# Loading the first slice of w1 as two column pieces on two queues, in a SiLU MLP's forward and backward kernel

## The chip, the cores and the metric

The kernel runs on one core of a Trainium2 chip. The metric is the device time of one execution in microseconds (us). The time before is the median of five executions, 322.19 us (320.18 to 322.25). One execution was profiled: it took 321.06 us by the same clock, and its trace spans 319.3 us from the first to the last instruction, so 1.76 us lie around the span.

## The reference

A two-layer network with a SiLU between, and its gradients for a given `grad_out`. All tensors are bfloat16; S = 2048 rows, D = 640, F = 1536.

```
def _fwd_reference(x, w1, w2):          # x [1, 2048, 640], w1 [640, 1536], w2 [1536, 640]
    h = jnp.einsum("bsd,df->bsf", x, w1)
    h = _silu(h)
    out = jnp.einsum("bsf,fd->bsd", h, w2)
    return out

def reference(x, w1, w2, grad_out):
    _out, _vjp = jax.vjp(_f, x, w1, w2)  # _f is _fwd_reference
    _grads = _vjp(grad_out)
    return (_out, *_grads)               # out, grad x, grad w1, grad w2
```

## The kernel before

All matmuls are 128 by 128 stationary tiles, with D as five tiles (`DT` = 5), F as twelve (`FT` = 12) and S as sixteen. The rows of x are worked through in four chunks of 512 (`SC`). For each chunk the kernel computes h transposed (F on the partitions), SiLU and its derivative, then the gradient that comes back through w2, and then two products that give the chunk of `out` and of grad x; the two weight gradients come at the end, after all chunks. TensorE does all of this in one long sequence.

The change touches only the start, where nothing is on the chip yet. Chunk 0 has its own routine, `h_first`. The first three 128-row tiles of x (`NQ` = 3, 160 KB each) are loaded as they lie, and TensorE turns them (`pe_x`, line 211) with 15 transposes. Their results are copied from PSUM into `xT` (line 216) by VectorE, ScalarE and VectorE again: D tile 0, then D tiles 1 and 2, then 3 and 4. The fourth x tile is transposed by a DMA (line 195).

Then `h_first` runs its matmuls in an order that follows the loading of w1 (line 251). For each D tile `dt_` in turn, it multiplies `xT[:, dt_, 0:384]` with the first eight F tiles (`NA` = 8, `FA` = 1024 columns). So the first eight matmuls read only D tile 0 of w1, columns 0 to 1023, that is "the first w1 slice"; the next eight read D tile 1, and so on. 40 such matmuls are followed by 40 short ones over the last 128 rows, and then by F tiles 8 to 11 in the usual order (line 220).

w1 therefore comes in pieces: for each D tile one transfer of 128 rows by 1024 columns (`load_w1`, line 188; 256 KB), and one transfer for columns 1024 to 1535 of all D tiles (line 196). w1 and w2 go into `w1_nat` and `w2_nat`; the profile calls both `w_nat`. It calls the slice's transfers L188, the x tiles' L185, and it counts the DMA instructions on the queue of the engine that issues them, SPq for SyncE and ACTq for ScalarE.

What sets the order of the issues is the order in the code, engine by engine. ScalarE issues x tile 1 and then the first w1 slice. SyncE issues x tiles 0 and 2, then the w1 slices of D tiles 1 to 4, then the transposing load of the fourth x tile (line 195), the rest of w1 (line 196), w2 (line 199), the transposed `grad_out` chunk (line 179), the three parts of w2 transposed (line 202) and w1 transposed (line 203). `start_before_entry_wait` moves every engine's instructions up to the last one in the list `early` ahead of the wait at the program's entry; on SyncE that list ends with the slice of D tile 2. A DMA instruction may also wait for an earlier transfer: the semaphores of transfers are used again, in turn.

Of the kernel before, what the change touches and what calls it, by code (L numbers as in the profile page):

```python
# [75 lines left out]
def kernel(  # L76
# [11 lines left out]
    nc = tc.nc  # L88
# [13 lines left out]
    FC = 512  # L102
# [7 lines left out]
    FA = NA * P  # L110
# [37 lines left out]
    with ExitStack() as mctx:  # L148
# [9 lines left out]
        early = [nc.vector.memset(warm[:], 1.0)]  # L158
# [25 lines left out]
        def load_x(eng, q):  # L184
            return eng.dma_start(out=x_nat[:, q, :], in_=x_v[:, q, :])  # L185

        def load_w1(k, cols=slice(0, F), eng=nc.sync):
            return eng.dma_start(out=w1_nat[:, k, cols], in_=w1_v[:, k, cols])  # L188

        early += [load_x(nc.sync, 0), load_x(nc.scalar, 1), load_x(nc.sync, 2)]  # L190
        early += [load_w1(0, slice(0, FA), nc.scalar)]
        early += [load_w1(k, slice(0, FA)) for k in range(1, 3)]
        for k in range(3, DT):
            load_w1(k, slice(0, FA))
# [288 lines left out]
```

## Time and profile before

| What | Value | Where from |
|---|---|---|
| median of five executions | 322.19 us | 320.18, 321.06, 322.19, 322.24, 322.25 |
| the profiled execution | 321.06 us | one of the five |
| its span | 319.3 us | first to last instruction of the trace |
| TensorE (PE) busy | 314.7 us, 99% of the span | busy time by engine |
| VectorE / ScalarE busy | 102.9 / 77.2 us | busy time by engine |
| mean rate of the DMA engines | 209 GB/s | 66.85 MB over the span |
| first w1 matmul (line 251) starts | 5.89 us | timeline |
| last one of line 251 ends | 14.79 us | chain of waits |

A row of the timeline gives the start from the span's beginning, the duration of the run of equal instructions, the engine, the line, the operation and its tiles, how many there were, and in brackets how long the engine had been idle and what released it. For a DMA the row is the issue, on its issuing engine's queue; when the data have landed is told separately, as the time from issue to landing. The 16 DMA engines are shared by all queues: q10 carries what ScalarE issues and q1 what SyncE issues, and the share of a queue is the time of its packets as a part of 16 engines' time.

### The profile page before, as it was taken

The numbers are of one execution on the slowest core, as the hardware profiler recorded it, in microseconds if no ns is written. First come the engines' busy times: TensorE is split into PE (matmuls) and PEld (weight loads), VectorE is DVE, ScalarE is ACT, GpSimd is POOL, SyncE is SP. The second block draws the span as 40 slices with busy tenths as digits, with TensorE's granted clock in tenths as the row PEclk, the third lists the DMA queues.
The fourth block names the chain that finished last, engine by engine and source line by source line (L and its number), as shares of the span: only waits on it lengthen the run. The fifth ranks groups of instructions, "written<-read, shape, count | busy, mean of one in ns | idle before, by whom it ended". The sixth has DMA issues, their size and how long they took to land.

```text
span 319.3 us, 3632 instructions
## 1 busy us (share of the span) xinstructions
PE 314.7 (99%) x1529; PEld 147.2 (46%) x1529; DVE 102.9 (32%) x182; ACT 77.2 (24%) x139; POOL 0.7 (0%) x6
## 2 busy tenths in 40 slices
PE   7999999999999999999999999999999999999997
PEld 5644444444444444444444444444444444444444
DVE  1388541477510087710147751000000110001001
ACT  2392001545201255411054520110100001001010
POOL 0000000000000000000000000000000000000000
PEclk9999999999999999999999999999999999999999
DMA  8999999999799684291635079909999999996011
GB/s 245 349 177 233 234 269 267 330 298 313 214 288 311 171 204 121 73 321 66 165 120 147 0 245 271 226 19 300 259 231 261 258 218 344 267 235 210 33 35 49
DMA packets 147120, 66.85 MB, mean 209 GB/s; under 512 B 113312, under 2 KB 146464, under 8 KB 147104
## 3 DMA queue, kind: packets, MB, share of 16 engines
q1 hardware_dynamic: 146816, 66.20, 81.6%
q10 hardware_dynamic: 288, 0.43, 0.4%
q8 instruction: 12, 0.20, 0.3%
q14 instruction: 4, 0.03, 0.0%
HBM read 9.18 MB, written 28.97 MB: 119 GB/s over the span
## 4 chain that ended last, share of the span: by engine, by line
PE 97%; DMA 2%; ACTq 0%; issue 0%; DVE 0%; DVEq 0%
PE hp L299 32%; PE hp L388 16%; PE hp L283 16%; PE hp L439 15%; PE hp L220 14%; PE hp L251 3%; DMA w_nat<-in_w_dram 2%; PE hp L419 1%; ACTq L185 0%; DVE g L430 0%; DVEq L430 0%; ACTq L467 0%
## 5 line engine op out<-in xcount | busy, mean ns | idle before, releaser
L283 PE MATMUL hp<-goT,w2T 128*128 128x512 bf16 x240 | 56.9, 379 | 0.0
L299 PE MATMUL hp<-aT,w_nat 128*128 128x512 bf16 x240 | 52.5, 379 | 0.0
L299 PE MATMUL hp<-ghT,w1T 128*128 128x512 bf16 x240 | 52.5, 379 | 0.0
L388 PE MATMUL hp<-a_blk,go_nat 128*128 128x512 bf16 x240 | 52.0, 379 | 0.0
L439 PE MATMUL hp<-gh_blk,x_nat 128*128 128x512 bf16 x224 | 48.5, 379 | 0.0
L220 PE MATMUL hp<-xT,w_nat 128*128 128x512 bf16 x200 | 48.2, 379 | 0.0
L307 ACT ACTIVATE oT<-hp 128x512 bf16<-128x512 f32 x24 | 14.4, 599 | 104.3 <-PE hp L299 104.3
L229 ACT ACTIVATE aT<-hp 128x512 bf16<-128x512 f32 x48 | 28.5, 613 | 38.4 <-PE hp L220 30.4
L299 PEld LDWEIGHTS <-w_nat 128*128 128x128 bf16 x240 | 23.5, 98 | 28.3
L299 PEld LDWEIGHTS <-w1T 128*128 128x128 bf16 x240 | 23.5, 98 | 28.3
L388 PEld LDWEIGHTS <-go_nat 128*128 128x128 bf16 x240 | 23.5, 98 | 28.3
L283 PEld LDWEIGHTS <-w2T 128*128 128x128 bf16 x240 | 23.5, 98 | 28.3
L290 DVE SCALAR_TENSOR_TENSOR ghT<-ghT,hp 128x512 bf16<-128x512 bf16 x48 | 32.5, 683 | 7.0 <-PE hp L283 7.0
L439 PEld LDWEIGHTS <-x_nat 128*128 128x128 bf16 x224 | 21.9, 98 | 26.4
L309 DVE CAST oT<-hp 128x512 bf16<-128x512 f32 x16 | 11.0, 691 | 70.6 <-PE hp L299 70.6
L236 DVE SCALAR_TENSOR_TENSOR ghT<-aT,v 128x512 bf16<-128x512 bf16 x48 | 32.6, 687 | 0.3
L220 PEld LDWEIGHTS <-w_nat 128*128 128x128 bf16 x200 | 19.5, 98 | 23.4
L235 DVE TENSOR_SCALAR v<-t 128x512 bf16<-128x512 f32 x48 | 20.1, 426 | 28.1 <-ACT t L233 28.1
L233 ACT ACTIVATE t<-hp 128x512 f32<-128x512 f32 x44 | 26.4, 618 | 0.0
L450 DVE CAST g<-hp 128x512 bf16<-128x512 f32 x7 | 4.8, 692 | 47.0 <-PE hp L439 28.5
L398 DVE CAST g2T<-hp 128x512 bf16<-128x512 f32 x7 | 4.8, 692 | 46.1 <-PE hp L388 46.1
L396 ACT ACTIVATE g2T<-hp 128x512 bf16<-128x512 f32 x8 | 4.8, 598 | 47.0 <-PE hp L388 47.0
(24 smaller groups left out, 42.1 us busy)
## 6 DMA issues: line engine op xcount, KB each, us to landing
aT_scr<-aT SPq DMA_DIRECT2D x4, 1536.0 KB, 6.7
ghT_scr<-ghT SPq DMA_DIRECT2D x4, 1536.0 KB, 7.9
out_dram<-o_sb SPq DMA_DIRECT2D x8, 640.0 KB, 3.4
oT_scr<-oT SPq DMA_DIRECT2D x4, 640.0 KB, 3.9
go_nat<-in_grad_out_dram SPq DMA_DIRECT2D x4, 640.0 KB, 7.6
gxT_scr<-oT SPq DMA_DIRECT2D x4, 640.0 KB, 4.8
w_nat<-in_w_dram SPq DMA_DIRECT2D x1, 1920.0 KB, 10.4
x_nat<-in_x_dram SPq DMA_DIRECT2D x3, 640.0 KB, 7.0
```

What stands on the lines that cost most here:

```text
L220: nc.tensor.matmul(hp[:], lhsT=w1_nat[:, dt_, ft * P:(ft + 1) * P], rhs=xT[:, dt_, :], start=(dt_ == 0), stop=(dt_ == DT - 1),)
L229: nc.scalar.activation(aT[:, ft, :], hp[:], ACT.Silu)
L233: nc.scalar.activation(t[:], hp[:], ACT.Tanh, scale=0.5)
L235: nc.vector.tensor_scalar(out=v[:], in0=t[:], scalar1=-0.5, scalar2=0.5, op0=ALU.mult, op1=ALU.add)
L236: nc.vector.scalar_tensor_tensor(out=ghT[:, ft, :], in0=aT[:, ft, :], scalar=1.0, in1=v[:], op0=ALU.subtract, op1=ALU.mult)
L283: nc.tensor.matmul(gp[:], lhsT=w2T[:, dt_, ft * P:(ft + 1) * P], rhs=goT[:, dt_, :], start=(dt_ == 0), stop=(dt_ == DT - 1),)
L290: nc.vector.scalar_tensor_tensor(out=ghT[:, ft, :], in0=ghT[:, ft, :], scalar=1.0, in1=gp[:], op0=ALU.add, op1=ALU.mult)
L299: nc.tensor.matmul(op_[:], lhsT=w_all[:, ft, dt_ * P:(dt_ + 1) * P], rhs=rhs_all[:, ft, :], start=(ft == 0), stop=(ft == FT - 1),)
L307: nc.scalar.activation(oT[:, dt_, :], op_[:], ACT.Copy)
L309: nc.vector.tensor_copy(out=oT[:, dt_, :], in_=op_[:])
L388: nc.tensor.matmul(gp[:], lhsT=go_nat[:, st, dt_ * P:(dt_ + 1) * P], rhs=a_blk[:, st, :], start=(st == 0), stop=(st == ST - 1),)
L439: nc.tensor.matmul(gp[:], lhsT=x_nat[:, st, dt_ * P:(dt_ + 1) * P], rhs=gh_blk[:, st, :], start=(st == 0), stop=(st == ST - 1),)
```

## The change

```
-        early += [load_w1(0, slice(0, FA), nc.scalar)]
+        early += [load_w1(0, slice(0, FC), nc.scalar), load_w1(0, slice(FC, FA))]
         early += [load_w1(k, slice(0, FA)) for k in range(1, 3)]
         for k in range(3, DT):
             load_w1(k, slice(0, FA))
```

`FC` is 512 and `FA` is 1024. The first slice, 128 rows by 1024 columns, becomes two transfers of 128 rows by 512 columns (128 KB each). Columns 0 to 511 stay on ScalarE's queue behind x tile 1. Columns 512 to 1023 go on SyncE's queue, behind x tile 2, which is the third x tile, and ahead of the slices of D tiles 1 to 4. Both are in the list `early`. No other transfer, no matmul and no copy is changed.

More of the change, by code (lines that the diff above doesn't have):

```diff
@@ L190 @@
         early += [load_x(nc.sync, 0), load_x(nc.scalar, 1), load_x(nc.sync, 2)]
-        early += [load_w1(0, slice(0, FA), nc.scalar)]
+        early += [load_w1(0, slice(0, FC), nc.scalar), load_w1(0, slice(FC, FA))]
         early += [load_w1(k, slice(0, FA)) for k in range(1, 3)]
```

## The prediction

> **What bounds the kernel now.** I read the chain of waits first, in order of time, then TensorE's own waits.
>
> ```profile
> 0.63 5.22 DMA w_nat<-in_w_dram
> 5.84 0.04 issue
> 5.89 8.91 PE hp L251 x80
> 14.79 4.32 PE hp L220 x20
> ```
>
> ```profile
> PE hp L251 <- DMA w_nat<-in_w_dram: 1.8, 1, 1.8
> PE wp L162 <- DVE warm L158: 0.5, 1, 0.5
> ```
>
> The reader is to see two things. From 5.89 us to the end TensorE (PE) waits for nothing: its list of waits has only these two entries, both ahead of that. So whatever moves the matmuls of line 251 earlier or later moves the end by as much, until some other load comes late. And what they wait for is one transfer, the first w1 slice: issued at 0.63, landed at 5.84.
>
> Was the other operand ready? The timeline around 4 us:
>
> ```profile
> 2.62 1.51 PE L211 MATMUL tp<-ident,x_nat 128*128 128x128 bf16 x15
> 3.95 0.82 DVE L216 COPY xT<-tp 128x384 bf16<-128x384 bf16 x2 [3.50 <-PE tp L211]
> 4.06 0.80 ACT L216 COPY xT<-tp 128x768 bf16<-128x768 bf16 x1 [1.37 <-PE tp L211]
> ```
>
> Yes. VectorE's first copy takes 0.36 us (the shorter of that group's two, 358 and 548 ns), so D tile 0 of x stands at 4.31 and all of it at 4.86. The w1 slice is 1.53 us later than its partner.
>
> Why so late? The DMA queues in two stretches, 2.4 to 3.8 us and 3.8 to 5.6 us (packets, MB, share of 16 engines):
>
> ```profile
> q10 hardware_dynamic: 144, 0.25, 56.9%
> q1 hardware_dynamic: 150, 0.21, 45.6%
> ...
> q1 hardware_dynamic: 237, 0.44, 81.3%
> q10 hardware_dynamic: 8, 0.01, 3.9%
> ```
>
> The slice is the last transfer on q10. Nearly all of it moved before 3.8 us; in the next 1.8 us only eight packets of q10 went. 128 rows over 16 engines are eight per engine, so I read the tail as one DMA engine that was held up and then shared its turns with q1. The transfer lands when that engine has finished.
>
> **What the change does, part by part.**
>
> *The half on ScalarE's queue.* Same issue slot (0.63), half the bytes. It lands at 5.84 at the latest if the engine is held up as before. At best it is ready before xT is, and F tiles 0 to 3 start at 4.31 + 0.04 = 4.35. The 40 long matmuls take 6.51 us (the stretch from 5.89 to 12.40), 0.163 each, so these four take 0.65 and the eight of one D tile 1.30. Before, D tile 1 began at 5.89 + 1.30 = 7.19; that is the point to compare with.
>
> *The half on SyncE's queue.* It takes the slot at 1.00 that D tile 1's slice had; every later issue of SyncE moves back one slot. The four slices were issued at 1.00, 1.48, 2.04 and 2.42 and took 5.1, 5.3, 5.3 and 5.6 us to land: 6.1, 6.8, 7.3 and 8.0. This is the row nearest to the new transfer: same queue, same place behind x tile 2, twice the bytes. Two bounds follow.
>
> - *Every slot lands as it did, whatever is in it.* The new half at 6.1, D tile 1 at 6.8. F tiles 4 to 7 run from 6.14 to 6.79, D tile 1 starts at 6.84: **0.35 us earlier** than 7.19.
> - *The bytes decide.* Ahead of D tile 1's slice there are the same bytes as before, so it lands at 6.1 still. The new half, ahead of it on the same queue, is there by then minus its successor's share; if it and the first half are ready by 4.8, D tile 1 starts at 6.14: **1.05 us earlier**. The far bound is xT alone, 4.35 + 1.30 = 5.65, or 1.54 earlier, which would need D tile 1's slice to land 0.5 us sooner than it did. I don't take that for the estimate; it marks the floor.
>
> *Costs.* The additional issue takes about the row's 0.43 us on SyncE (slots 0.47 apart) and holds up nobody but SyncE's own later loads. Moved by 0.47, with TensorE 1.05 earlier, they stand thus. D tiles 2, 3 and 4 in the next slots (7.3, 8.0, some 8.7) against needs at 7.44, 8.74 and 10.04. The transposed fourth x tile, 2.95 + 5.8 + 0.47 = 9.2, against 11.35. The rest of w1, 4.29 + 6.4 + 0.47 = 11.2, against 13.6. All are covered, D tile 2 by a tenth only; if that cover is gone, its lateness comes off the gain and no more. The rows of the packets are shorter: 1280-byte packets cost 54 ns (182 packets at 102% of 16 engines over 0.6 us) and 2048-byte ones 84 ns (124 at 93% over 0.7 us), so I estimate 45 ns for 1024 bytes. 256 x 45 / 16 = 0.72 us instead of 128 x 84 / 16 = 0.67: 0.05 us, inside the bounds.
>
> *The wait that moves.* SyncE's queue itself waits once in this stretch:
>
> ```profile
> SPq L199 <- DMA w_nat<-in_w_dram: 1.0, 1, 1.0
> ```
>
> The load of w2 was held until the first slice had landed, a transfer's semaphore being used again eight transfers later. With one transfer more, each reuse falls on another partner: this wait goes to another load, and the transposing loads behind it in the queue (lines 179, 202, 203) move with it by up to a microsecond either way. I cost that at nothing: w2 landed at 5.86 + 10.4 = 16.3 and is needed at 18.95 - 1.05 = 17.9; w1 transposed landed at 27.1 + 11.1 = 38.2 and is needed at 45.01 - 1.05 = 44.0. Without this cover it would cost that microsecond.
>
> **The sum.** Between 0.35 and 1.05 I take the middle, 0.70, since the new half has half the bytes of the slot's old tenant but cannot be quicker than its own slowest engine. The profiled execution, 321.06 (span 319.3), would become 320.36. It lies 1.13 below the median of the runs, so for the median I move 322.19 by the same amount: **321.5 us**.
>
> [...]
>
> **The rivals.**
>
> *B: the held-up engine stays where it is (no gain).* A column split gives every engine its eight rows in both pieces, so an engine that stalls early stalls the q10 half as well. For it: the tail was on q10, whose slot does not change. Against it: half the bytes are left behind the stall, and the tail's packets shared turns with q1. Then F tiles 0 to 3 start at 5.89 and nothing is won as long as the second half lands by 6.5: 322.2.
>
> *C: the second half becomes the late one (slower).* Place: F tile 4 of D tile 0. It decides from a landing at 7.19 - 0.65 - 0.04 = 6.50, only 0.4 beyond the slot's 6.1. Price: if the tail seen on q10 (from 3.8 to 5.84, 2.0 us) falls on this half on top of its slot, it lands at 8.1, D tile 1 starts at 8.79, **1.6 us late: 323.8** from the median. For it: two transfers have two chances of a slow engine, and SyncE's queue is the one with three others ahead and behind. [...] Against it: four slices in this queue landed an orderly 0.6 to 0.7 us apart.
>
> [...]
>
> *D: the slow runs lose their delay (much faster).* The five times are 320.18, 321.06 and three at 322.2. If the upper level is the first slice landing another microsecond later, which nothing would hide, the bound of D tile 1's slice cuts it off, and all runs go to about 321.06 - 1.05 = 320.0, or 320.5 with the smaller gain. For it: the levels are as far apart as the wait is long. Against it: only one execution is traced, and what the others waited for isn't seen.
>
> **How the numbers follow.** The forecast 0.47 (321.1 to 321.8), B 0.19, C 0.18, D 0.16. About 0.5%, or 1.61 us, is what a measurement of this kernel can tell from no change: faster is below 320.58, slower above 323.80. Faster: D, and 0.08 of the forecast, for a median that falls on the lower level: 0.24. Slower: 0.15 of C, which has its price at that mark and more if the clock drops too. Same: 0.61. The range goes from 319.9 (D with a full gain) to 323.0 (half of C's price), which leaves out some 0.15 at the top and little below.
>
> **What would show it.** Right: line 251's first matmul at 4.4 to 5.3 us, the eighth ending at 6.8 or before, D tile 1's at 6.1 to 6.9, no later wait on TensorE's list. Wrong by B: the first at 5.8 again. By C: TensorE idle twice, the longer time ahead of F tile 4. By D: the five times of the changed kernel within half a microsecond. My reading of the tail is wrong if q10 still shows packets after 4 us with half the slice on it.

## The result and the profile after

The changed kernel took 320.11 us (median of 43 executions, 319.41 to 322.50) and the kernel before 320.86 us (median of 80, 319.53 to 323.19). The ratio of their means (320.20 and 321.15) is 0.997, 95% interval 0.9958 to 0.9982: a gain of 0.3%, or 0.6 to 1.4 us. The median of 322.19 shown at first came from five executions and was not the kernel's level.

The times show more than their medians. Those of the kernel before lie in two groups with nothing between: 51 from 319.5 to 321.1 (median 320.36) and 29, or 36%, from 321.9 to 323.2 (median 322.44). Of the changed kernel's 43, two lie in the upper group, and the others have a median of 320.06. So the change took 0.3 us off an ordinary execution and removed nearly all of a 2 us delay that befell 29 executions of 80. (The kernel before ran 71 times more beside the experiments below; 17 of these were above 321.5 us.)

The profiled execution of the changed kernel took 320.38 us, span 318.6. Its chain of waits over the first 20 us (start, us, what):

```profile
0.51 2.10 PE wp L162 x18
2.61 0.01 issue
2.62 1.78 PE tp L211 x15
4.40 0.02 issue
4.42 9.69 PE hp L251 x80
14.12 4.32 PE hp L220 x20
```

The load that stood in this chain (5.22 us of it) is gone. TensorE goes from the warm-up matmuls to the transposes to line 251 and sets its own pace from 0.51 us on. Its list of waits has one entry left:

```profile
PE wp L162 <- DVE warm L158: 0.5, 1, 0.5
```

The two pieces landed at 0.62 + 3.2 = 3.8 us (ScalarE's queue) and 0.99 + 3.2 = 4.2 (SyncE's), where the whole slice had landed at 5.84. The DMA queues in the two stretches shown of before, 2.4 to 3.8 us (first two lines) and 3.8 to 5.6 us (last line):

```profile
q1 hardware_dynamic: 312, 0.37, 76.0%
q10 hardware_dynamic: 153, 0.14, 29.2%
...
q1 hardware_dynamic: 364, 0.66, 101.1%
```

q10 has no packet left after 3.8 us, so the tail of eight is gone, and q1 moved 0.66 MB in the second stretch instead of 0.44.

But line 251 starts 1.47 us sooner (4.42, not 5.89) and ends only 0.67 us sooner. Its 80 matmuls take 9.69 us instead of 8.91. The long ones, by form, in the kernel before, and in the changed one from 4.8 to 5.9 us and from 6.3 to 11 us (busy us, mean ns of one):

```profile
L251 PE MATMUL hp<-xT,w_nat 128*128 128x384 bf16 x40 | 6.7, 326 | 1.8 <-DMA w_nat<-in_w_dram 1.8
```

```profile
L251 PE MATMUL hp<-xT,w_nat 128*128 128x384 bf16 x5 | 1.8, 517 | 0.0
...
L251 PE MATMUL hp<-xT,w_nat 128*128 128x384 bf16 x31 | 5.3, 328 | 0.0
```

The first of the changed kernel's long matmuls run at half pace. Each has a weight load ahead of it, and these show the step from one matmul to the next (the rows of the weight loads, PEld, around 5.5 us):

```profile
5.02 0.15 PEld L251 LDWEIGHTS <-w_nat 128*128 128x128 bf16 x1 [0.17 <-issue]
5.34 0.15 PEld L251 LDWEIGHTS <-w_nat 128*128 128x128 bf16 x1 [0.17 <-issue]
5.66 0.15 PEld L251 LDWEIGHTS <-w_nat 128*128 128x128 bf16 x1 [0.17 <-issue]
5.98 7.96 PEld L251 LDWEIGHTS <-w_nat 128*128 128x128 bf16 x74 [0.17 <-issue]
```

They follow each other at 0.32 us, against 0.163 in the trace of before. The pace doubles near 6 us, all at once. In the trace of before it had doubled during the transposes (their durations fell from 314 to 219 ns by 3.7 us), so that line 251 ran at full pace, 326 ns a long matmul, from its start. The profile's row of the granted clock shows nothing of this, it reads full from its first slice in both; the durations are the evidence.

### The profile page after: what moved, and what is told of

Same layout as the page of the kernel before. It is cut to its first block, busy times and chain, and to the rows that moved or that the text cites. A ratio compares the mean times of both kernels' runs of the same rounds, so it can differ in the third digit from the quotient of the medians.

```text
span 318.6 us, 3633 instructions
## 1 busy us (share of the span) xinstructions
PE 315.8 (99%) x1529; PEld 147.7 (46%) x1529; DVE 103.0 (32%) x182; ACT 77.2 (24%) x139; POOL 0.7 (0%) x6
## 4 chain that ended last, share of the span: by engine, by line
PE 99%; DVE 0%; issue 0%; DVEq 0%
PE hp L299 33%; PE hp L388 16%; PE hp L283 16%; PE hp L439 15%; PE hp L220 14%; PE hp L251 3%; PE hp L419 1%; PE wp L162 1%; PE tp L211 1%; DVE g L430 0%; DVE warm L158 0%; DVEq L430 0%; DVEq L467 0%
```

## The experiments

Two theories were to be told apart. *Landing*: the upper group consists of executions in which the first slice lands later still. *Clock*: it consists of executions in which TensorE's full clock comes late, because of the idle hole in front of line 251. And the change has two parts, the split and the move to the other queue.

**Filling the hole in the kernel before.**

```
+            for i in range(14):
+                nc.tensor.matmul(hs[0][:, 0:P], lhsT=warm[:], rhs=warm[:], start=True, stop=True)
             for dt_ in range(DT):
```

> The kernel before, with 14 idle matmuls (128 columns, result unused) between the transposes and the first w1 matmul, so that TensorE stays busy while the first slice is on its way. The 80 times of the kernel before lie in two groups: 51 up to 321.1 us (median 320.36) and 29 from 321.9 us (median 322.44). Clock theory: the upper group are executions in which TensorE's full clock is granted late because the idle hole of 1.75 us lowers its activity. Then the upper group shrinks from 36% to 10% or less and the median becomes 320.3 to 320.6, though the first slice lands no sooner and line 251 still starts near 5.9 us. Landing theory: the upper group are executions in which the first slice lands a further microsecond or two late. Then the fill changes nothing: upper group 36%, median 320.8 to 321.0.

Measured: 321.12 us, 12 executions, eleven from 320.65 to 321.47 and one far off at 333.7, with a granted clock of 0.95; the kernel before beside it 320.58, 8 of 29 in the upper group. Ratio 1.0008 (0.999 to 1.0026). No other execution lies in the upper group, as the clock theory has it, but the median missed both forecasts. Probably the fillers hold up the executions in which the slice lands early; none of these was traced. In the profile the slice landed at 5.58, line 251 started at 5.62 and ran at full pace (326 ns).

**Putting the hole back into the changed kernel**, its loads untouched, first long and then shorter.

```
+            nc.vector.tensor_copy(out=late[:], in_=xT[:, DT - 1, 0:P])
+            for _ in range(4):                       # 1 in hole_short
+                nc.vector.tensor_scalar(out=late[:], in0=late[:], scalar1=-0.5, scalar2=0.5, op0=ALU.mult, op1=ALU.add)
+            nc.vector.tensor_copy(out=late_b[:], in_=late[:])
+            nc.tensor.matmul(hs[0][:, 0:P], lhsT=warm[:], rhs=late_b[:], start=True, stop=True)
             for dt_ in range(DT):
```

> The changed kernel, with a chain of VectorE instructions behind the last x copy that TensorE has to wait for ahead of its first w1 matmul: all loads stay early, but the idle hole of the kernel before is put back (line 251 starts near 5.9 us instead of 4.4). Clock theory: the two groups of times come back, about a third of the executions near 322.4 us, median 320.4 to 321.0. Landing theory: the loads are early, so there is one group only, the changed kernel's times moved up by the hole: median 320.06 + 1.4 = 321.5, at most 5% above 322.5, and no second group 2 us apart.

Measured: 323.46 us, six executions, 323.15 to 324.3; ratio 1.0087 (1.0059 to 1.0114). The hole came out longer than meant (2.22 us, line 251 at 6.69) and neither forecast held: one group, but 1.1 us beyond 320.06 plus the 2.27 us of later start. In its profile ten long matmuls ran at half pace, up to 9.9 us, against five in the profile of after, which is 0.8 us of that.

> The changed kernel with a shorter idle hole than in hole_after: one VectorE step in place of four, so that line 251 starts near 5.9 us as in the profile of the kernel before (idle 1.4 to 1.5 us). hole_after held TensorE to 6.63 us and its matmuls ran at half pace to 9.9 us; all its six times lay in one group at 323.5. Clock theory: at this length the full clock comes in time in some executions and not in others: two groups, one near 321.2, one near 322.9, a third to two thirds in the upper, spread 1.5 us or more. Landing theory: the loads are early in all executions, so one group at 321.5 with no more spread than the changed kernel has (1.2 us).

Measured: 322.78 us, eight executions: 320.71, 320.91, 320.99, and five from 322.69 to 324.15. Ratio 1.0054 (1.0023 to 1.0085). Two groups, five of eight in the upper, where the landing theory had a single one. In the profiled execution (323.51, of the upper group) the two pieces landed at 4.7 and 5.1 us, well ahead of line 251; here are its TensorE waits, and then its long matmuls by form from 6.8 to 9.6 us:

```profile
PE hp L265 <- DVE late_b L264: 1.4, 1, 1.4
PE tp L211 <- DMA x_nat<-in_x_dram: 0.9, 1, 0.9
PE wp L162 <- DVE warm L158: 0.5, 1, 0.5
```

```profile
L251 PE MATMUL hp<-xT,w_nat 128*128 128x384 bf16 x9 | 3.1, 524 | 0.0
```

After a hole of 1.4 us, ten matmuls ran at half pace (nine of them start before 9.6 us). In this execution the first x tile was late by 0.9 us as well, which is why line 251 starts at 6.75; that part of its time is a late load, not the clock.

**Taking the warm-up away from the changed kernel** (`NWARM = 18` becomes 1).

> The changed kernel with 1 warm-up matmul (line 162) instead of 18; loads, transposes and all else as they are. [...] Landing theory: nothing that is waited for changes: 319.9 to 320.3.

Measured: 320.90 us, 320.29 to 321.76; ratio to the kernel before 0.9997 (0.9977 to 1.0017), so the gain of the change is given up, and the median lies above the landing theory's 319.9 to 320.3. Line 251 starts at 4.41 as ever, but its long matmuls still took 518 ns on average between 4.8 and 6.9 us. The full pace came at 7.0 us in this trace, near 6 in that of after. The loads were as in the changed kernel, so what differs is the pace.

**Further traces of the kernel before**, to catch one of the upper group.

> The kernel before once more, for a second trace of it. If its time falls in the upper group (36%), clock theory: the matmuls of line 251 start by 6 us but are 480 to 527 ns each instead of 326 until 8.4 us or later. Landing theory: line 251 starts at 7 us or later at 326 ns each. In the lower group: start between 4.4 and 5.9, 326 ns from the start or soon after.

> A further trace of the kernel before, as look_a, to have one of each group.

> A third further trace of the kernel before; look_a and look_b were both of the lower group (320.85 and 319.80). If the time is 321.9 or more, clock theory: line 251 starts by 6 us, its matmuls 480 to 527 ns each until 8.4 us or later. Landing theory: start at 7 us or later, 326 ns each.

> A fourth further trace of the kernel before, with the same expectation of each theory as look_c, in case that one is of the lower group too.

Measured: 320.85, 319.80, 322.48 and 324.26 us. The last two are of the upper group; for each the chain of waits and then the long matmuls by form, first look_c (6.3 to 8.4 us), then look_d (6.5 to 11.2 us):

```profile
0.54 4.64 DMA x_nat<-in_x_dram
5.18 0.05 issue
5.23 0.71 PE tp L211 x5
5.94 0.02 issue
5.96 10.25 PE hp L251 x80
```

```profile
L251 PE MATMUL hp<-xT,w_nat 128*128 128x384 bf16 x8 | 2.7, 518 | 0.0
```

```profile
0.61 5.78 DMA w_nat<-in_w_dram
6.39 0.05 issue
6.44 11.54 PE hp L251 x80
```

```profile
L251 PE MATMUL hp<-xT,w_nat 128*128 128x384 bf16 x15 | 5.0, 526 | 1.8 <-DMA w_nat<-in_w_dram 1.8
```

Both theories have a share. Something is late in both (the third x tile at 5.18, the first slice at 6.39) and leaves a hole, but line 251 starts only 0.07 and 0.55 us after that of the profile shown of before (5.89). The larger part is its length: 10.25 and 11.54 us against 8.91, all of it half pace. Of look_d's 3.20 us over 321.06, 0.55 is the later start and 2.63 the half pace. look_a (320.85) had the third x tile late too, with a hole of 1.3 us, but its long matmuls took 326 ns, the full pace; look_b (319.80) had its slice by 4.4 us and no wait at all. In these five traces a late load is the occasion; whether the full pace comes in time then decides between the groups.

The traces also hold a record of the granted clock itself, in eight of the 14 profiles. In each it begins where the pace doubles, for instance at 3.71 us in before, 4.88 in look_b, 6.09 in after and 11.82 in look_d. In look_d TensorE had been idle twice by then, for 0.23 us ahead of the transposes and for 1.83 ahead of line 251; in before the hole of 1.75 us came behind the grant. That such holes put off the grant fits these traces. They are not the whole of it, since look_b and after have no hole and differ by 1.2 us, and what decides the moment of the grant isn't shown.

**The parts alone.** The split without the move:

```
-        early += [load_w1(0, slice(0, FC), nc.scalar), load_w1(0, slice(FC, FA))]
+        early += [load_w1(0, slice(0, FC), nc.scalar), load_w1(0, slice(FC, FA), nc.scalar)]
```

> The split without the move: both column pieces on ScalarE's queue, the other w1 slices in SyncE's old slots. If the split alone does it (F tiles 0 to 3 wait for half the bytes): first w1 matmul at 4.4 us, median 320.1 to 320.3, upper group under 10%. If it is the move to SyncE's queue that helps (the second half lands ahead of D tile 1's slice in the same queue instead of sharing turns with it): TensorE waits ahead of F tile 4, median 320.5 to 320.9, upper group 15 to 36%.

Measured: 320.72 us, 319.87 to 322.22, two of twelve above 321.5; ratio 1.0004 (0.9981 to 1.0027). The profile, from 4 us on:

```profile
4.48 1.44 PE L251 MATMUL hp<-xT,w_nat 128*128 128x384 bf16 x4
6.07 8.29 PE L251 MATMUL hp<-xT,w_nat 128*128 128x384 bf16 x76 [0.15 <-DMA w_nat<-in_w_dram]
```

Four matmuls start early, at half pace, and the fifth (F tile 4) waits for the second piece until 6.07. This is rival C's place, though not on SyncE's queue. The second forecast fits, and the split alone shows no gain.

The move without the split:

```
-        early += [load_w1(0, slice(0, FC), nc.scalar), load_w1(0, slice(FC, FA))]
+        early += [load_w1(0, slice(0, FA))]
```

> The move without the split: the whole first slice (256 KB) on SyncE's queue behind x tile 2 and ahead of the other w1 slices. If it was the sharing of turns between the two queues that kept the tail late, it lands near 4.2 us as the second half does in the changed kernel (4.17), line 251 starts at 4.4, and the median is 320.1 to 320.3. If the split is what counts, it lands as late as before (5 to 6 us) and the median is 320.6 to 320.9 with the upper group at 36%.

Measured: 320.41 us, nine of twelve from 320.21 to 320.60, three from 321.82 to 322.44; ratio 0.9992 (0.9968 to 1.0017). The profiled one (321.82) is of the upper group; its chain of waits, and its long matmuls from 5.25 to 8 us:

```profile
0.99 3.86 DMA w_nat<-in_w_dram
4.86 0.05 issue
4.90 10.62 PE hp L251 x80
```

```profile
L251 PE MATMUL hp<-xT,w_nat 128*128 128x384 bf16 x10 | 3.4, 524 | 0.7 <-DMA w_nat<-in_w_dram 0.7
```

The slice is there by 4.86, a microsecond sooner than in the profile of before, and the execution is still 0.76 us slower than that one, at half pace until past 8 us after a hole of only 0.7. This is the plainest evidence for the clock. Neither forecast fits: the slice landed between the two, and the median lies between theirs. With 12 executions against 29, neither part by itself is shown to gain, nor is a gain excluded (the intervals reach down to 0.998 and 0.997); the two together do gain, in the 43 against 80.

**The changed kernel again, and with two warm-up matmuls more** (`NWARM = 20`).

> The changed kernel with 20 warm-up matmuls instead of 18, to close the idle 0.28 us between them and the first transpose. [...] If the two further matmuls hold up the transposes in executions in which x lands at 2.3 us: the same or 0.1 us more, 320.1 to 320.2.

> The changed kernel itself once more, beside warm20_after on the same chip, and for a second trace. Median 319.9 to 320.3, upper group 5% or less; line 251 starts at 4.4 us with no wait for a load, first column piece landing near 3.85 and second near 4.1 to 4.5.

Measured: 319.94 us (319.60 to 320.69; ratio 0.9976, 0.9952 to 0.9999) and 320.03 us (319.53 to 320.68; ratio 0.9984, 0.9967 to 1.0001), none of the 24 in the upper group, where the kernel before beside them had 5 of 23. The 0.09 us between them is within their spread, so it stays open whether 20 is better than 18. In after_again line 251 started at 4.76, because the third x tile landed at 4.0: the forecast of 4.4 missed by that.

**One sum over all profiles.** The first matmul of the usual order (line 220 of the kernel before) starts at 14.63 us in the profile of before and at 13.96 in that of after. Taken from the execution's time that leaves 306.4 in both. Over all 14 profiles, of all versions, it leaves 306.41 to 306.51, though the times go from 319.8 to 324.3. So everything that differs happens ahead of that matmul: the start of line 251 and the pace of its matmuls.

## Why the prediction was right and wrong

- *What bounds the kernel.* Right: the remainder of 306.4 us shows that a microsecond at the start is a microsecond at the end.
- *The tail on q10.* Right in its place: with half the slice on it, q10 was empty after 3.8 us in the profile of after, and after 4 us in five of the six profiles with the changed loads (in hole_short its x tiles were late). The packet records of before fit the reading: one packet of q10 lasted 0.97 us from 3.04 us, against 0.084 for most, and the last ones started 0.16 us apart. Of the 16 landings counted on the slice's semaphore 15 came by 4.13 us and the last at 5.84. Which engine took a packet isn't recorded, so that one engine was held up stays a reading. But it isn't always w1's slice. In the five traces of before the slice landed at 4.4, 5.3, 5.7, 5.8 and 6.4 us, and in two of them it was the third x tile that was late. What holds up an engine wasn't tried.
- *The new half takes its slot's landing, 6.1.* Too pessimistic: it landed at 4.2, with D tile 1's slice at 1.46 + 4.4 = 5.9. The bytes are not the whole reason, since in whole_sync the full 256 KB in that slot landed at 4.86. By the loads alone D tile 1 could have started at 5.9, a gain of 1.3.
- *The sum of 0.70.* The profiled executions differ by 0.68 us, and D tile 1 started at 6.52 where the sum has 7.19 - 0.70 = 6.49. It was luck. The step "The 40 long matmuls take 6.51 us" took the full pace of the one traced execution for granted, so a later full pace was a term at nothing. The start came 1.47 us sooner and 0.78 was given back at half pace. Landing bounds and half pace happened to cancel.
- *The step that failed* is the next one: "for the median I move 322.19 by the same amount: 321.5 us". Three of those five executions were of the upper group, which holds 36% of 80; the level was 320.86. This is 1.33 of the 1.39 us between 321.5 and 320.11. That the medians differ by 0.75, near the 0.70 of the sum, is luck again: an ordinary execution gained 0.3, and the rest is the upper group that went. The likeliest case was called no change by the bound of 0.5%; over so many executions the gain of 0.3% is clear of no change.
- *Rival D* saw the two levels and that the change would remove the upper one. Its cause, the slice landing another microsecond late, was only part of it; half pace was the larger part in both traces of that group. (Its 320.5 for the smaller gain should be 321.06 - 0.35 = 320.7.) Rival C's chance of a slower kernel counts on more "if the clock drops too". No run here shows a hole that takes the full pace away: the hole of 1.75 us in before came after the full pace had been granted, at 3.71 us, and the matmuls behind it ran at 326 ns, while the holes that cost more than their length all came ahead of the grant. Getting the full pace was what mattered: without a hole it came near 6 us in after and near 5 in look_b, with a hole of 0.7 us at 8.4 in whole_sync, and with one of 1.8 us at 11.8 in look_d.
- *The waits that move.* Costed at nothing, and nothing it was, but the cover named is nearly used up. The wait at line 199 is gone, since w2 now takes over the semaphore of the third x tile, landed at 3.46 us. So w2 was issued 0.5 us sooner, yet it landed later, at 18.2 us; the changed kernel around that time:

```profile
18.23 0.36 PEld L299 LDWEIGHTS <-w_nat 128*128 128x128 bf16 x3 [0.29 <-DMA w_nat<-in_w_dram]
18.27 0.59 PE L299 MATMUL hp<-aT,w_nat 128*128 128x512 bf16 x2
```

The weight load of line 299 waited 0.29 us for it, hidden behind the matmul still running. A start half a microsecond sooner would meet this load next, in an execution in which it is as late: over the 14 profiles it landed between 15.7 and 18.2 us.

## What to carry to other kernels

Look at the times one by one before taking their median as a level: two groups with a gap ask for a mechanism that comes in some executions and not in others, and one profile shows only one of the two cases. At the start of this kernel an idle hole could cost more than its length: in hole_after line 251 started 2.27 us later and the time rose by 3.4 us, ten long matmuls instead of five being at half pace. Compare the durations of equal matmuls, because the clock row may not show it: here it read full throughout in before and after. Look at the last packets of a load: in the profile of before eight of them held up the slice by 2 us. In the six profiles with the two pieces on two queues these landed at 3.8 to 4.7 and 4.1 to 5.1 us, in the six with one piece on ScalarE's queue at 4.4 to 6.4; how much of that is the smaller size and how much the other queue isn't shown.

## What the runs showed that was not expected

The full pace came at about 3.7, 6 and 11.8 us in the traces of before, after and look_d, which all started TensorE at 0.5 us; the first and the last are the same kernel. The third x tile, 160 KB issued at 0.54 us, landed between 3.2 and 5.2 us over the 14 profiles. And the load of w2 landed 2.0 us later in the profile of after though it was issued 0.5 us earlier, 18.2 against 16.2 us; what held it up wasn't tried.
